# The first seven microseconds of a fused attention and mixer kernel: warm-up, tile 0 and the first weights rearranged

## The chip, the cores and the metric

The kernel runs on one core of a Trainium2 chip. A core has a matrix engine (TensorE; PE in the profile, with its weight loads as PEld), a vector engine (VectorE, DVE), a scalar engine (ScalarE, ACT), a general engine (GpSimd, POOL) and a sync engine (SyncE, SP), which here only issues DMAs. Each engine works through its own instructions in order and waits on semaphores for the others. Sixteen DMA engines move data. SBUF is the on-chip memory of 128 partitions, PSUM the accumulator memory of eight banks that TensorE writes. The metric is the time of one execution on the device in microseconds; lower is better.

## The reference

The input x has 2048 rows of 512 numbers in bf16. Each row is normalised (xn), and two branches work on xn; the output is x plus both.

```python
xn = layernorm(x)
# A: 32 heads of 16; each position attends to 8 positions, 2 apart, backwards
q, k, v = split(xn @ wqkv)
out_A = softmax(q . k[s - 2w] * 0.25 over w = 0..7) . v[s - 2w]  @ wo
# B: gated mixer with 688 + 688 channels
z = gelu(xn @ w_in);  z1 = z[:, :688];  z2 = layernorm(z[:, 688:])
g = w_sp @ z2 + b_sp[:, None]          # w_sp is 2048 x 2048
out_B = (z1 * g) @ w_out
return x + out_A + out_B
```

## The kernel before

The 2048 rows are 16 tiles of 128. The order of each engine's instructions is written out by hand, in five lists of short names (`pe`, `act`, `dve`, `pool`, `sp`) at the end of the kernel; `op_(name, after, f)` says what a name does and what it comes after, and the tile framework puts in the semaphore waits. No planner reorders anything.

**Front, per tile i.** SP loads x (`x0` to `x12`, line 163; tiles 0 to 5 one by one, then 2, 4 and 4 tiles). VectorE takes the statistics (`b`, line 170; `ag`, line 173), GpSimd turns the variance into a reciprocal root in two instructions (`gr`, lines 176 and 177), VectorE normalises (`n`, line 180; tile 0 in two halves of columns `n0a`, `n0`, line 184). For tiles 0 to 7 TensorE transposes xn in four 128x128 pieces into a bank of PSUM (`T`, line 213), ScalarE copies it to SBUF (`Tc`, line 216), and TensorE multiplies it by the 688 columns of the input weights that belong to z2 (`z`, line 231: 2 halves of 344 columns, 4 pieces of the contraction each, so eight matmuls). ScalarE applies gelu (`h`, line 249). Tiles 8 to 15 are transposed by DMA from SP's queue (`t`, line 196).

Tile 0 is cut finer: `T0a` and `T0` transpose two pieces each, into one bank; `Tc0a` and `Tc0` copy them; `z0a` and `z0A` do the first half of the columns (contraction pieces 0, 1 and 2, 3), `z0B` the second half.

**PSUM.** Three double banks `mm` and two single ones `aux` are handed out in turn; a user waits for the reader of the one before it. The transposes use `aux`, the products `mm`.

**What comes first.** VectorE clears a tile of zeros `warm` (line 129) and some small ones; nine matmuls of that tile with itself (`wu`, line 455) run on TensorE before tile 0 is there. ScalarE's queue issues the z2 weights in two DMAs `wz0` and `wz1` (line 239), one for each half of the columns, 688 bytes a piece. A clear of two numbers of that weight tile (line 142) makes `wz0` wait for VectorE; `wz1` stands behind it in the same queue. GpSimd issues the DMA of the bias (`b16`, line 245). Its transpose `B` (line 459) and copy `Bc` (line 461) turn it into a column of 16 numbers per partition; `B` stands between `T7` and `z6` in TensorE's list. The first block of the spatial weights (`W0`, line 451) reuses the memory of the zeros and so waits for `wu`.

**After the front** TensorE does the first z1 products `y`, the rest of z2, then q, k and v (line 324), the rest of z1, the spatial product (`M`, line 467), and the two output products (lines 511, 516 and 523), while VectorE works through the attention of the heads.

Of the kernel before, what the change touches and what calls it, by code (L numbers as in the profile page):

```python
# [7 lines left out]
BF16 = mybir.dt.bfloat16  # L8
# [5 lines left out]
P = 128  # L14
S = 2048
D = 512
NT = S // P
# [3 lines left out]
W = 8  # L21
# [5 lines left out]
FH = 688  # L27
F = 2 * FH
FHALF = FH // 2
# [13 lines left out]
def kernel(  # L43
# [12 lines left out]
    nc = tc.nc  # L56
    V = nc.vector
    A = nc.scalar
    G = nc.gpsimd
    PE = nc.tensor  # L60
# [9 lines left out]
    ident = sb.tile([P, P], BF16, name="ident")  # L70
# [12 lines left out]
    b16 = sb.tile([NT, P], BF16, name="b16")  # L83
    b_col = sb.tile([P, NT], F32, name="b_col")
# [7 lines left out]
    w_z = [wts[:, C * (3 * D + n * FH):C * (3 * D + (n + 1) * FH)].rearrange("p (k f) -> p k f", k=C) for n in (1, 0)]  # L92
# [13 lines left out]
    z2 = z2_r[:].rearrange("p (i f) -> p i f", i=NT)  # L106
# [9 lines left out]
    wsp_r = [wsp_all[:, n * NT * 2 * P:(n + 1) * NT * 2 * P] for n in range(3)]  # L116
# [4 lines left out]
    ph.append([wsp_r[2], z1_r[:, NT * D:NT * D + PU // 2]])  # L121
    ph.append([wsp_r[2], wts[:, 0:PU // 2]])
    BUF = dict(zip([(c, th) for c in range(NC) for th in range(2)], (0, 1, 2, 0, 1, 3, 0, 1)))
    warm = wsp_r[0][:, 0:D]

    mm = [ps.tile([P, 2, D], F32, name=f"mm{n}") for n in range(3)]
    aux = [ps.tile([P, D], F32, name=f"aux{n}") for n in range(2)]

    V.memset(warm, 0.0)  # L129
    V.memset(mhalf[:], -0.5)  # L130
    V.memset(eps_t[:], EPS)
    G.memset(ident[:], 0.0)
# [6 lines left out]
        V.memset(k_c[c][0:H, :, 0, 0:HALO], 0.0)  # L139
    V.memset(vp[0:H, :, 0, 0:HALO], 0.0)  # L140

    V.memset(w_z[1][0:1, 0, 0:2], 0.0)

    wq_d = A_wqkv.rearrange("(k p) f -> p k f", p=P)
    wi_d = B_w_in.rearrange("(k p) f -> p k f", p=P)
# [4 lines left out]
    def op_(name, after, f):  # L150
        assert name not in do, name
        do[name], needs[name] = f, list(after)

    def tok(i):
        return f"Tc{i}" if i < NPE else f"t{i}"
# [45 lines left out]
    def psum(kind, writer, reader, after, f):  # L201
        pool = mm if kind == "mm" else aux
        n = len(ring[kind])
        t = pool[n % len(pool)]
        old = [ring[kind][n - len(pool)]] if n >= len(pool) else []
        ring[kind].append(reader)
        op_(writer, list(after) + old, lambda: f(t))
        return t

    def turn(i, t, cs=range(C)):  # L210
        pt = t[:].bitcast(BF16)[:, 0:D]
        for c in cs:
            PE.transpose(pt[:, c * P:(c + 1) * P], xn[i % 8][:, c * P:(c + 1) * P], ident[:])  # L213

    def turned(i, t, c0=0, c1=C):
        A.copy(xnT[:, c0:c1, i * P:(i + 1) * P], t[:].bitcast(BF16)[:, c0 * P:c1 * P].rearrange("p (c t) -> p c t", c=c1 - c0))  # L216

    def make_T0():
        t = psum("aux", "T0a", "Tc0", ["n0a"], lambda t: turn(0, t, (0, 1)))
        op_("T0", ["T0a", "n0"], lambda: turn(0, t, (2, 3)))  # L220
        op_("Tc0a", ["T0a"], lambda: turned(0, t, 0, 2))
        op_("Tc0", ["T0"], lambda: turned(0, t, 2, 4))

    def make_T(i):
        t = psum("aux", f"T{i}", f"Tc{i}", [f"n{i}"], lambda t: turn(i, t))
# [3 lines left out]
    def z_half(t, i, part, hh, kcs=range(C)):  # L229
        for kc in kcs:  # L230
            PE.matmul(t[:, hh, 0:FHALF], xnT[:, kc, i * P:(i + 1) * P], w_z[part][:, kc, hh * FHALF:(hh + 1) * FHALF],  # L231
                      start=(kc == 0), stop=(kc == C - 1))

    def z_part(t, i, part):
        for hh in range(2):
            z_half(t, i, part, hh)

    for hh in range(2):
        op_(f"wz{hh}", [], lambda hh=hh: A.dma_start(  # L239
            w_z[1][:, :, hh * FHALF:(hh + 1) * FHALF], wi_d[:, :, FH + hh * FHALF:FH + (hh + 1) * FHALF]))  # L240
    op_("wk", [], lambda: SP.dma_start(w_k, wq_d[:, :, D:2 * D]))
    op_("wq", [], lambda: SP.dma_start(w_q, wq_d[:, :, 0:D]))
    op_("wv", [], lambda: SP.dma_start(w_v, wq_d[:, :, 2 * D:3 * D]))
# [3 lines left out]
    def z2_gelu(i, t):  # L247
        total = {"accum_out": zsum[:, i:i + 1]} if i in ZACT else {}
        A.activation(z2[:, i, :].rearrange("p (a b) -> p a b", a=2), t[:, :, 0:FHALF], ACT.Gelu_apprx_tanh, **total)  # L249
# [1 line left out]
    ZACT = range(8, NT)  # L251

    def make_z(i):
        t = psum("mm", f"z{i}", f"h{i}", [tok(i), "wz0", "wz1"], lambda t: z_part(t, i, 1))
        op_(f"h{i}", [f"z{i}"], lambda: z2_gelu(i, t))

    def make_z0():
        t0 = psum("mm", "z0a", "h0", ["Tc0a", "wz0"], lambda t: z_half(t, 0, 1, 0, (0, 1)))
        op_("z0A", ["z0a", tok(0)], lambda: z_half(t0, 0, 1, 0, (2, 3)))
        op_("z0B", ["z0A", "wz1"], lambda: z_half(t0, 0, 1, 1))  # L260
        op_("h0", ["z0B"], lambda: z2_gelu(0, t0))

    def z2_bn(i):
        for hh in range(2):
# [36 lines left out]
    for i in range(NT):  # L301
        g = i // 4 * 4
# [47 lines left out]
    last = {}  # L350
# [25 lines left out]
    for c, th in BUF:  # L376
        n = f"{c}{th}"
# [63 lines left out]
    USES = [f"y{i}" for i in range(NT)] + [f"{a}{p}" for a in "qkv" for p in range(8)]  # L441
# [8 lines left out]
    def load_wsp(n):  # L450
        SP.dma_start_transpose(wsp[n % 3], B_w_sp[n * 2 * P:(n + 1) * 2 * P, :])

    for n in range(8):
        op_(f"W{n}", [["wu"], [], ["HW"]][n] if n < 3 else [f"M{2 * n - 5}"], lambda n=n: load_wsp(n))
    op_("wu", [], lambda: [PE.matmul(aux[1][:], warm[:, 0:P], warm, start=True, stop=True) for _ in range(9)])

    def make_B():
        def turn_b(t):
            PE.transpose(t[:].bitcast(BF16)[:, 0:NT], b16[:], ident[0:NT, 0:NT])
        t = psum("aux", "B", "Bc", ["b16"], turn_b)  # L460
        op_("Bc", ["B"], lambda: A.copy(b_col[:], t[:].bitcast(BF16)[:, 0:NT]))

    def mix(t, j):
        w = wsp[(j // 2) % 3]
# [22 lines left out]
    def load_wo(g):  # L487
        SP.dma_start(wo_r[32 * g:32 * g + 32], A_wo.rearrange("(h d) n -> h d n", d=DH))
# [4 lines left out]
            SP.dma_start(wout[r:r + FREST, MF, :], B_w_out[MF * P:FH, :])  # L493

    for g in range(4):
        op_(f"LO{g}", [n for n in USES if n[0] != "y"] + [f"z{i}" for i in range(1, NT)] + ["z0B", last[3]], lambda g=g: load_wo(g))
    op_("LO4", USES, load_wout)
    LO = [f"LO{g}" for g in range(5)]
    for th in range(2):
# [59 lines left out]
    for n, c in enumerate(halves):  # L559
        i = groups[3][3]  # L560
# [1 line left out]
        op_(f"Sl{n}", [f"Fl{n}"], lambda n=n, c=c: (SP, A)[n].dma_start(out2[i * P:(i + 1) * P, c], o_of(i)[:, c]))  # L562


    pe = """wu T0a T0 z0a z0A T1 z0B T2 z1 T3 z2 T4 z3 T5 z4 T6 z5 T7 B z6 z7 y0 y1 z8 z9 z10 z11 z12 z13 z14
        k0 k1 q0 q1 z15 k2 k3 q2 q3 k4 k5 q4 q5 k6 k7 q6 q7
        v0 v1 v2 v3 v4 v5 v6 v7 y2 y3 y4 y5 y6 y7 y8 y9 y10 y11 y12 y13 y14 y15
        M0 M1 M2 M3 M4 M5 M6 M7 M8 M9 M10 M11 M12 M13 M14 M15
# [1 line left out]
    for n in pe:  # L570
        a, x = n[0], n[1:]
        if n in do:
            continue
        if n == "T0a":
            make_T0()
        elif a == "T":
            make_T(int(x))
        elif n == "z0a":
            make_z0()
        elif a == "z":  # L580
            make_z(int(x))
        elif a == "y":
            make_y(int(x))
        elif a in "qkv":
            make_heads(a, int(x))
        elif a == "M":
            make_M(int(x))
        elif a == "B":
            make_B()
    op_("GL", [], lambda: A.preload_act_table(ACT.Gelu_apprx_tanh))  # L590
    op_("EL", ["yg15"], lambda: A.preload_act_table_set("natural_log_exp_and_others"))

    act = """wz0 wz1 GL Tc0a Tc0 Tc1 Tc2 h0 Tc3 h1 Tc4 h2 Tc5 h3 Tc6 h4 Tc7 Bc h5 h6 h7 yg0 yg1 h8 h9 sq8 h10 h11 sq9 h12 h13 h14 sq10
        kc0 sq11 kc1 qc0 sq12 qc1 h15 kc2 sq13 kc3 sq14 qc2 sq15 qc3 kc4 kc5 qc4 qc5 kc6 kc7 qc6 qc7
        vc0 zn8 vc1 zn9 vc2 zn10 vc3 zn11 vc4 zn12 vc5 zn13 vc6 zn14 vc7 zn15
        yg2 yg3 yg4 yg5 yg6 yg7 yg8 yg9 yg10 yg11 yg12 yg13 yg14 yg15 EL
        G0 e0 G1 i0 e1 G2 i1 G3 G4 G5 G6 G7 G8 G9 G10 G11 G12 G13 G14 G15""".split()
    act += [f"E{i}" for n in (0, 1) for i in groups[n]]
    dve = """b0 ag0 b1 ag1 n0a n0 b2 ag2 n1 b3 ag3 n2 b4 ag4 n3 b5 ag5 n4 b6 ag6 b7 n5""".split()
    for i in range(6, NT):  # L600
        dve += [f"ag{i + 1}"] * (i + 1 < NT) + [f"b{i + 2}"] * (i + 2 < NT) + [f"n{i}"]
    dve += """zt0 zt1 zt2 zt3 zt4 zt5 zn0 zn1 zn2 zn3 zt6 zt7 zn4 zn5 zn6 zn7
# [62 lines left out]
```

## Time and profile before

| | us |
|---|---|
| median of three runs | 201.43 |
| lowest and highest of the three | 201.35, 202.9 |
| the profiled execution, whole | 201.17 |
| its span, first to last instruction | 199.4 |
| TensorE busy in the span | 194.3 |
| VectorE busy | 177.5 |
| ScalarE busy | 89.7 |
| GpSimd busy | 39.0 |

The span leaves out what comes before the first and after the last instruction, which is why it is shorter than the profiled execution. Times in the timeline count from the start of the span. In a row of the timeline the first number is the start, the second the length; what follows an arrow in square brackets is what ended the idle time before the instruction. A row with x4 stands for four instructions of one kind next to each other. Matmuls are pipelined, so a row's length includes the drain of its last one, and rows of TensorE overlap.

### The profile page before, as it was taken

To read this page: it belongs to the slowest core of one execution; us is meant where nothing else is said; L and a number is where in the kernel's file an instruction comes from. 1 tells how busy PE (TensorE), PEld (TensorE's weight loads), DVE (VectorE), ACT (ScalarE), POOL (GpSimd) and SP (SyncE) were. 2 spreads that over 40 slices of the span, in tenths; PEclk is the share of its full clock that TensorE was granted. 3 is DMA by queue.
4 is the path that set the end of the run, shared out by engine and by line. 5 is a ranking of instruction groups with operands and counts; after the bars stand their busy time and mean duration, and the time that the engine had idled before them with its cause. 6 is when DMAs were issued, how large, how long until landed. Compare 5 with 4: busy or idle time off the path is not lost.

```text
span 199.4 us, 4530 instructions
## 1 busy us (share of the span) xinstructions
PE 194.3 (97%) x1935; PEld 122.5 (61%) x1935; DVE 177.5 (89%) x204; ACT 89.7 (45%) x130; POOL 39.0 (20%) x67
## 2 busy tenths in 40 slices
PE   7899999999999999999999999999999999999993
PEld 2576666666777766666666666666666654443441
DVE  4999895899898999988999999999999999997234
ACT  2597797795559996672542311112221110043000
POOL 5677122002999330330000000000000000000000
PEclk9999999999999999999999999999999999999999
DMA  5999476840977999998099999999996679914233
GB/s 163 349 361 230 89 123 139 144 81 0 196 132 140 197 196 147 185 167 168 11 234 229 188 168 227 237 123 258 198 230 60 118 219 233 154 19 133 81 105 105
DMA packets 68964, 32.58 MB, mean 163 GB/s; under 512 B 56912, under 2 KB 67024, under 8 KB 68816
## 3 DMA queue, kind: packets, MB, share of 16 engines
q1 hardware_dynamic: 65568, 24.12, 59.5%
q0 software_dynamic: 2176, 7.40, 20.0%
q10 hardware_dynamic: 1200, 0.77, 1.4%
q8 instruction: 15, 0.25, 0.5%
q14 instruction: 5, 0.04, 0.1%
HBM read 10.03 MB, written 2.10 MB: 61 GB/s over the span
## 4 chain that ended last, share of the span: by engine, by line
PE 95%; DMA 3%; DVE 1%; ACTq 0%; DVEq 0%; issue 0%
PE mm L467 37%; PE mm L324 21%; PE mm L231 19%; PE mm L523 7%; PE mm L511 7%; DMA wts<-in_B_w_in_dram 3%; PE aux L511 2%; PE mm L516 1%; PE aux L213 1%; ACTq L239 0%; DVE z L561 0%; DVEq L660 0%; DVE wsp L129 0%; PE aux L523 0%; DVE qk L139 0%
## 5 line engine op out<-in xcount | busy, mean ns | idle before, releaser
L467 PE MATMUL mm<-z,wsp 128*128 128x344 bf16 x512 | 74.8, 309 | 0.0
L467 PEld LDWEIGHTS <-wsp 128*128 128x128 bf16 x512 | 50.1, 98 | 24.6
L324 PE MATMUL mm<-xnT,wts 128*32 128x512 bf16 x768 | 41.9, 380 | 0.0
L231 PE MATMUL mm<-wts,xnT 128*128 128x344 bf16 x256 | 39.0, 309 | 0.5 <-ACT xnT L216 0.5
L324 PEld LDWEIGHTS <-wts 128*32 128x32 bf16 x768 | 29.5, 140 | 12.0 <-issue 0.6
L425 DVE TENSOR_TENSOR prod<-vp,a_sb 128x4096 bf16<-128x4096 bf16 x16 | 36.1, 2285 | 0.0
L481 ACT ACTIVATE qk<-mm,b_col 128x688 bf16<-128x688 f32 x16 | 13.3, 830 | 45.3 <-PE mm L467 38.3
L231 PEld LDWEIGHTS <-xnT 128*128 128x128 bf16 x256 | 24.4, 98 | 13.0 <-issue 1.0
L358 DVE TENSOR_TENSOR prod<-qk 128x4096 bf16<-128x4096 bf16 x12 | 27.0, 2288 | 1.8 <-DMA qk<-qk 1.6
L429 DVE TENSOR_TENSOR prod<-prod,prod 128x8192 bf16<-128x8192 bf16 x6 | 26.5, 4420 | 0.0
L337 ACT CAST qk<-mm 128x1024 bf16<-128x1024 f32 x16 | 16.2, 1012 | 7.8 <-PE mm L324 7.8
L313 ACT ACTIVATE z<-mm 128x688 bf16<-128x688 f32 x16 | 11.8, 748 | 5.7 <-PE mm L231 5.3
L366 POOL DMA_DIRECT2D prod<-prod x10 | 8.7, 1022 | 28.3 <-DVE zvar L282 16.0
L523 PE MATMUL mm<-wts,xnT 32*128 32x512 bf16 x192 | 14.2, 374 | 0.0
L511 PEld LDWEIGHTS <-qk 128*128 128x128 bf16 x85 | 8.2, 98 | 9.4 <-issue 0.8
L511 PE MATMUL mm<-wts,qk 128*128 128x512 bf16 x60 | 13.6, 379 | 0.0
L249 ACT ACTIVATE z<-mm 128x688 bf16<-128x688 f32 x16 | 11.9, 745 | 1.9 <-PE mm L231 1.8
L170 DVE BATCH_NORM_STATS2 stats<-z 128x6 f32<-128x512 bf16 x16 | 10.8, 673 | 1.7 <-DMA z<-in_A_x_dram 1.7
L523 PEld LDWEIGHTS <-xnT 32*128 32x128 bf16 x256 | 6.3, 93 | 7.7 <-issue 0.8
L556 DVE TENSOR_TENSOR z<-mm,wsp 128x512 bf16<-128x512 f32 x6 | 3.8, 684 | 8.0 <-PE mm L523 4.8
L550 ACT CAST z<-mm 128x512 bf16<-128x512 f32 x6 | 3.2, 598 | 13.7 <-PE mm L523 12.3
L177 POOL TENSOR_TENSOR rstd<-rstd,mhalf 128x1 f32<-128x1 f32 x16 | 9.0, 561 | 1.3
(82 smaller groups left out, 169.6 us busy)
## 6 DMA issues: line engine op xcount, KB each, us to landing
prod<-prod POOLq DMA_DIRECT2D x10, 512.0 KB, 7.6
wts<-in_A_wo_dram SPq DMA_DIRECT2D x4, 512.0 KB, 6.3
wsp<-in_A_x_dram SPq DMA_DIRECT2D x2, 1024.0 KB, 6.5
out_dram<-z SPq DMA_DIRECT2D x15, 128.0 KB, 1.8
wts<-in_A_wqkv_dram SPq DMA_DIRECT2D x3, 512.0 KB, 8.6
z<-in_A_x_dram SPq DMA_DIRECT2D x2, 512.0 KB, 6.4
wsp<-z POOLq DMA_DIRECT2D x2, 512.0 KB, 6.5
wsp<-wts POOLq DMA_DIRECT2D x2, 512.0 KB, 8.9
```

What stands on the lines that cost most here:

```text
L231: PE.matmul(t[:, hh, 0:FHALF], xnT[:, kc, i * P:(i + 1) * P], w_z[part][:, kc, hh * FHALF:(hh + 1) * FHALF], start=(kc == 0), stop=(kc == ...
L249: A.activation(z2[:, i, :].rearrange("p (a b) -> p a b", a=2), t[:, :, 0:FHALF], ACT.Gelu_apprx_tanh, **total)
L313: op_(f"yg{i}", [f"y{i}"], lambda: A.activation(z1u[:, i, 0:FH].rearrange("p (a b) -> p a b", a=2), t[:, :, 0:FHALF], ACT.Gelu_apprx_tanh))
L324: PE.matmul(t[32 * g:32 * g + 32, dd, :], w, r, start=(kc == 0), stop=(kc == C - 1), tile_position=(0, 32 * g))
L337: op_(f"{a}c{p}", [f"{a}{p}"], lambda: A.copy(home(a, p), t[:].rearrange("p d (t s) -> p d t s", t=2)))
L358: V.tensor_tensor(pr, q, k, ALU.mult)
L425: return lambda: V.tensor_tensor(dst, vp[:, :, th, off:off + GS], a_sb[:, th, W - 1 - w].unsqueeze(1).broadcast_to([P, DH, GS]), ALU.mult)
L429: return lambda: V.tensor_tensor(dst, dst, x, ALU.add)
L467: PE.matmul(t[:, hh, 0:FHALF], w[:, k, (j % 2) * P:(j % 2 + 1) * P], z2[:, k, hh * FHALF:(hh + 1) * FHALF], start=(k == 0), stop=(k == NT ...
L481: lambda: A.activation(gs[j % 3].rearrange("p (a b) -> p a b", a=2), t[:, :, 0:FHALF], ACT.Identity, bias=b_col[:, j:j + 1]))
L511: PE.matmul(po[i][:, c], uT[th][:, m, t0:t0 + P], wout[:, m, c], start=(start and m == 0), stop=(stop and m == MF - 1))
L523: PE.matmul(po[groups[n][g]], op[32 * g:32 * g + 32, th, d, s * P:(s + 1) * P], wo_r[32 * g:32 * g + 32, d, :], start=(start and d == 0), ...
```

## The change

- **Warm-up.** The tile of zeros and its clear go. The warm-up multiplies a constant of ones that the framework holds, one number per partition read with stride zero, ten times instead of nine. Three more such products, of 128 columns (`wd`), come after tile 0's transposes. `W0` no longer comes after `wu`.
- **Tile 0 in two banks.** `T0a` and `T0` write one `aux` bank each, and `Tc0a` and `Tc0` read one each.
- **z2's weights by rows.** `wz0` brings contraction pieces 0 and 1 of all 688 columns, `wz1` pieces 2 and 3: pieces of 1376 bytes. `z0a` now does pieces 0 and 1 of both halves of columns, `z0b` pieces 2 and 3. The clear that holds the weights covers 128 partitions by 512 columns of the first piece.
- **Bias.** `B` stands right behind `T0`, ahead of `wd` and `z0a`, and uses a bank of `mm`; `Bc` stands behind `Tc0`. The products `z1` to `z15` come after `Bc`.
- **VectorE's list.** `b3 ag3 n2` becomes `b3 n2 ag3`.

```diff
-    warm = wsp_r[0][:, 0:D]
+    ones = nc.const_aps.tensor(1.0, [P, D], BF16)
...
-    V.memset(warm, 0.0)
...
-    V.memset(w_z[1][0:1, 0, 0:2], 0.0)
+    V.memset(w_z[1][:, 0, 0:D], 0.0)
...
-        t = psum("aux", "T0a", "Tc0", ["n0a"], lambda t: turn(0, t, (0, 1)))
-        op_("T0", ["T0a", "n0"], lambda: turn(0, t, (2, 3)))
-        op_("Tc0a", ["T0a"], lambda: turned(0, t, 0, 2))
-        op_("Tc0", ["T0"], lambda: turned(0, t, 2, 4))
+        t0 = psum("aux", "T0a", "Tc0a", ["n0a"], lambda t: turn(0, t, (0, 1)))
+        t1 = psum("aux", "T0", "Tc0", ["T0a", "n0"], lambda t: turn(0, t, (2, 3)))
+        op_("Tc0a", ["T0a"], lambda: turned(0, t0, 0, 2))
+        op_("Tc0", ["T0"], lambda: turned(0, t1, 2, 4))
...
-    for hh in range(2):
-        op_(f"wz{hh}", [], lambda hh=hh: A.dma_start(
-            w_z[1][:, :, hh * FHALF:(hh + 1) * FHALF], wi_d[:, :, FH + hh * FHALF:FH + (hh + 1) * FHALF]))
+    for n in range(2):
+        op_(f"wz{n}", [], lambda n=n: A.dma_start(w_z[1][:, 2 * n:2 * n + 2, :], wi_d[:, 2 * n:2 * n + 2, FH:F]))
...
-        t = psum("mm", f"z{i}", f"h{i}", [tok(i), "wz0", "wz1"], lambda t: z_part(t, i, 1))
+        t = psum("mm", f"z{i}", f"h{i}", [tok(i), "wz0", "wz1", "Bc"], lambda t: z_part(t, i, 1))
...
-        t0 = psum("mm", "z0a", "h0", ["Tc0a", "wz0"], lambda t: z_half(t, 0, 1, 0, (0, 1)))
-        op_("z0A", ["z0a", tok(0)], lambda: z_half(t0, 0, 1, 0, (2, 3)))
-        op_("z0B", ["z0A", "wz1"], lambda: z_half(t0, 0, 1, 1))
-        op_("h0", ["z0B"], lambda: z2_gelu(0, t0))
+        t0 = psum("mm", "z0a", "h0", ["Tc0a", "wz0"], lambda t: [z_half(t, 0, 1, hh, (0, 1)) for hh in range(2)])
+        op_("z0b", ["z0a", tok(0), "wz1"], lambda: [z_half(t0, 0, 1, hh, (2, 3)) for hh in range(2)])
+        op_("h0", ["z0b"], lambda: z2_gelu(0, t0))
...
-        op_(f"W{n}", [["wu"], [], ["HW"]][n] if n < 3 else [f"M{2 * n - 5}"], lambda n=n: load_wsp(n))
-    op_("wu", [], lambda: [PE.matmul(aux[1][:], warm[:, 0:P], warm, start=True, stop=True) for _ in range(9)])
+        op_(f"W{n}", [[], [], ["HW"]][n] if n < 3 else [f"M{2 * n - 5}"], lambda n=n: load_wsp(n))
+
+    def spin(t, cols, count):
+        for _ in range(count):
+            PE.matmul(t[:, 0:cols], ones[:, 0:P], ones[:, 0:cols], start=True, stop=True)
+
+    op_("wu", [], lambda: spin(aux[1], D, 10))
+    op_("wd", ["T0"], lambda: spin(mm[1][:, 0, :], P, 3))
...
-        t = psum("aux", "B", "Bc", ["b16"], turn_b)
-        op_("Bc", ["B"], lambda: A.copy(b_col[:], t[:].bitcast(BF16)[:, 0:NT]))
+        t = mm[2][:, 0, :]
+        op_("B", ["b16", "T0"], lambda: turn_b(t))
+        op_("Bc", ["B"], lambda: A.copy(b_col[:], t.bitcast(BF16)[:, 0:NT]))
...
-    pe = """wu T0a T0 z0a z0A T1 z0B T2 z1 T3 z2 T4 z3 T5 z4 T6 z5 T7 B z6 z7 y0 y1 z8 z9 z10 z11 z12 z13 z14
+    pe = """wu T0a T0 B wd z0a T1 z0b T2 z1 T3 z2 T4 z3 T5 z4 T6 z5 T7 z6 z7 y0 y1 z8 z9 z10 z11 z12 z13 z14
...
-    act = """wz0 wz1 GL Tc0a Tc0 Tc1 Tc2 h0 Tc3 h1 Tc4 h2 Tc5 h3 Tc6 h4 Tc7 Bc h5 h6 h7 yg0 yg1 h8 h9 sq8 h10 h11 sq9 h12 h13 h14 sq10
+    act = """wz0 wz1 GL Tc0a Tc0 Bc Tc1 Tc2 h0 Tc3 h1 Tc4 h2 Tc5 h3 Tc6 h4 Tc7 h5 h6 h7 yg0 yg1 h8 h9 sq8 h10 h11 sq9 h12 h13 h14 sq10
...
-    dve = """b0 ag0 b1 ag1 n0a n0 b2 ag2 n1 b3 ag3 n2 b4 ag4 n3 b5 ag5 n4 b6 ag6 b7 n5""".split()
+    dve = """b0 ag0 b1 ag1 n0a n0 b2 ag2 n1 b3 n2 ag3 b4 ag4 n3 b5 ag5 n4 b6 ag6 b7 n5""".split()
```

More of the change, by code (lines that the diff above doesn't have):

```diff
@@ L453 @@
     for n in range(8):
-        op_(f"W{n}", [["wu"], [], ["HW"]][n] if n < 3 else [f"M{2 * n - 5}"], lambda n=n: load_wsp(n))
-    op_("wu", [], lambda: [PE.matmul(aux[1][:], warm[:, 0:P], warm, start=True, stop=True) for _ in range(9)])
+        op_(f"W{n}", [[], [], ["HW"]][n] if n < 3 else [f"M{2 * n - 5}"], lambda n=n: load_wsp(n))
[4 more added lines that the diff above has]
+    op_("wd", ["T0"], lambda: spin(mm[1][:, 0, :], P, 3))
     def make_B():
         def turn_b(t):
-            PE.transpose(t[:].bitcast(BF16)[:, 0:NT], b16[:], ident[0:NT, 0:NT])
-        t = psum("aux", "B", "Bc", ["b16"], turn_b)
-        op_("Bc", ["B"], lambda: A.copy(b_col[:], t[:].bitcast(BF16)[:, 0:NT]))
+            PE.transpose(t.bitcast(BF16)[:, 0:NT], b16[:], ident[0:NT, 0:NT])
+        t = mm[2][:, 0, :]
+        op_("B", ["b16", "T0"], lambda: turn_b(t))
+        op_("Bc", ["B"], lambda: A.copy(b_col[:], t.bitcast(BF16)[:, 0:NT]))
     def mix(t, j):
@@ L495 @@
     for g in range(4):
-        op_(f"LO{g}", [n for n in USES if n[0] != "y"] + [f"z{i}" for i in range(1, NT)] + ["z0B", last[3]], lambda g=g: load_wo(g))
+        op_(f"LO{g}", [n for n in USES if n[0] != "y"] + [f"z{i}" for i in range(1, NT)] + ["z0b", last[3]], lambda g=g: load_wo(g))
     op_("LO4", USES, load_wout)
```

## The prediction

> **What bounds the kernel now.** I read the page first, then the chain of waits in order of time, then who made TensorE wait, and last the timeline of the first 13 us, where the change lies. The page:
>
> ```profile
> span 199.4 us, 4530 instructions
> PE 194.3 (97%) x1935; PEld 122.5 (61%) x1935; DVE 177.5 (89%) x204; ACT 89.7 (45%) x130; POOL 39.0 (20%) x67
> PE 95%; DMA 3%; DVE 1%; ACTq 0%; DVEq 0%; issue 0%
> ```
>
> TensorE is busy 194.3 of 199.4 us and 95% of the chain is its own work. A cut in the front is worth what it takes off the start of TensorE's unbroken work, no more. The chain (start, length, what) shows where that starts:
>
> ```profile
> 1.97 5.26 DMA wts<-in_B_w_in_dram
> 7.27 0.74 PE mm L231 x4
> 8.01 0.37 PE aux L213 x4
> ...
> 15.11 0.22 PE aux L213 x4
> ...
> 184.55 3.77 PE mm L523 x65
> ```
>
> ```profile
> 15.33 0.11 PE aux L459
> 15.45 5.65 PE mm L231 x38
> ```
>
> ```profile
> PE mm L231 <- ACT xnT L216: 0.5, 1, 0.5
> ```
>
> The second weight transfer lands at 7.23 and releases z0B at 7.27; from there the chain is TensorE alone. The wait of 0.5 is z0a's, for the copy of tile 0. The bias transpose (L459) is 0.11 us of the solid part. The chain makes the weights look like the limit. The timeline of the front corrects this (start, length, engine, line):
>
> ```profile
> 0.86 0.27 DVE L129 MEMSET wsp<- 128x256 uint32 x1 [0.86 <-PEq L649]
> ...
> 1.19 4.02 PE L455 MATMUL aux<-wsp 128*128 128x512 bf16 x9 [1.19 <-DVE wsp L129]
> ...
> 1.39 0.06 DVE L142 MEMSET wts<- 1x1 uint32 x1
> ...
> 1.67 0.68 POOL L245 DMA_DIRECT2D b<-in_B_b_sp_dram  x1
> ...
> 4.80 0.60 DVE L184 TENSOR_SCALAR z<-z,mv,rstd 128x256 bf16<-128x256 bf16 x2 [0.20 <-POOL rstd L177]
> ...
> 5.20 0.54 PE L213 MATMUL aux<-ident,z 128*128 128x128 bf16 x4
> ...
> 5.32 0.69 DVE L170 BATCH_NORM_STATS2 stats<-z 128x6 f32<-128x512 bf16 x1
> 5.78 0.65 ACT L216 COPY xnT<-aux 128x256 bf16<-128x256 bf16 x2 [1.97 <-PE aux L213]
> ...
> 6.14 0.38 DVE L180 TENSOR_SCALAR z<-z,mv,rstd 128x512 bf16<-128x512 bf16 x1
> ...
> 6.21 0.76 PE L231 MATMUL mm<-wts,xnT 128*128 128x344 bf16 x4 [0.46 <-ACT xnT L216]
> ...
> 6.65 0.55 POOL L177 TENSOR_TENSOR rstd<-rstd,mhalf 128x1 f32<-128x1 f32 x1
> ...
> 6.72 0.69 DVE L170 BATCH_NORM_STATS2 stats<-z 128x6 f32<-128x512 bf16 x1 [0.20 <-DMA z<-in_A_x_dram]
> ...
> 7.45 0.18 DVE L173 BATCH_NORM_AGGREGATE mv<-stats 128x2 f32<-128x6 f32 x1
> 7.55 0.38 DVE L180 TENSOR_SCALAR z<-z,mv,rstd 128x512 bf16<-128x512 bf16 x1
> ...
> 7.85 0.69 DVE L170 BATCH_NORM_STATS2 stats<-z 128x6 f32<-128x512 bf16 x1
> ...
> 7.99 0.40 PE L213 MATMUL aux<-ident,z 128*128 128x128 bf16 x4
> 8.06 0.55 POOL L177 TENSOR_TENSOR rstd<-rstd,mhalf 128x1 f32<-128x1 f32 x1
> ...
> 8.67 0.39 DVE L180 TENSOR_SCALAR z<-z,mv,rstd 128x512 bf16<-128x512 bf16 x1
> ...
> 9.39 0.39 PE L213 MATMUL aux<-ident,z 128*128 128x128 bf16 x4
> ...
> 9.79 0.39 DVE L180 TENSOR_SCALAR z<-z,mv,rstd 128x512 bf16<-128x512 bf16 x1
> ...
> 11.50 0.40 DVE L180 TENSOR_SCALAR z<-z,mv,rstd 128x512 bf16<-128x512 bf16 x1
> ...
> 12.17 0.39 PE L213 MATMUL aux<-ident,z 128*128 128x128 bf16 x4
> ...
> 14.87 11.09 SPq L196 DMA_TRANSPOSE xnT<-z  x8
> ```
>
> Tile 2's normalisation n2 (DVE, 7.55) ends at 7.93 and T2 starts at 7.99, 0.06 behind it. So T2 waits for VectorE: weights that land earlier only move the idle time from before z0B to before T2. VectorE in turn is held by x's third tile: b3 starts at 6.72 after waiting 0.20 for a DMA. The front has two chains that end together; the change shortens TensorE's, and touches VectorE's in two places.
>
> **The change part by part.**
>
> *Warm-up and clears.* The clear of the warm-up tile (0.27) goes; the clear that holds the weights grows from one word (0.06) to the same 128x256 words as the one that goes, so I price it at 0.27. The last clear ended at 1.45 and now ends at about 1.45 - 0.27 + 0.21 = 1.39: the weights' issue moves by less than 0.1, which I take as nothing. Ten spins cost 4.02 x 10/9 = 4.47 in place of 4.02, but need no clear: if TensorE starts when VectorE did, at 0.86, they end at 5.33, against T0a at 5.20. T0a may be 0.13 late, which the slack below takes up. No row has spins on a constant that is read with stride zero: bounds are nothing, and, were each to take twice as long, 4.5 us; I take nothing, as the row of 512 columns is nearest.
>
> *Two banks.* The copy of tile 0 starts at 5.78, after all four transposes (5.20 + 0.54). With a bank of its own the first half can follow the first pair, about 0.27 sooner, and z0a could start at 5.94 in place of 6.21. But B is now queued ahead of it on TensorE, and waits for the bias:
>
> ```profile
> b<-in_B_b_sp_dram POOLq DMA_DIRECT2D x1, 4.0 KB, 4.2
> ```
>
> It was issued at 1.67 and landed at about 5.87. Behind B in TensorE's queue stand the three short spins of wd (128 columns each, priced from four transposes in 0.22 of the chain: 0.17) and then z0a: 5.87 + 0.05 + 0.11 + 0.17 = 6.20. So the banks give nothing while the bias lands at 5.87; wd and the moved B cost nothing. Bounds: 0.27 gained if the bias came at 5.5, as much lost if it came at 6.1.
>
> *Weights by rows.* The queue tables of two stretches, 3.3 to 6.5 us (weights and x together) and 9.6 to 10.7 us (only packets of 1376 B), give packets, MB and share of 16 engines:
>
> ```profile
> q10 hardware_dynamic: 1007, 0.67, 69.9%
> q1 hardware_dynamic: 399, 0.37, 35.2%
> ```
>
> ```profile
> q1 hardware_dynamic: 315, 0.43, 106.3%
> ```
>
> The first pair adds up to over 100%: the engines are full. A 688 B packet takes 0.699 x 16 x 3.2 / 1007 = 35.5 ns, one of 1376 B 1.063 x 16 x 1.1 / 315 = 59.4 ns. 1024 of the former are now 512 of the latter: 36.4 - 30.4 = 6.0 us of engine time, 0.37 us over 16 engines. So what shares the engines with them, x2 and x3, and the weights, may land up to 0.37 sooner: wz1 at 6.86 to 7.23, x3 at 6.3 to 6.7. z0b starts at 6.20 + 0.59 (four of the eight matmuls of 1.17 us) + T1 0.22 = 7.01 or later and needs 0.59, so it ends about 7.6, ahead of T2.
>
> *VectorE's order b3 n2 ag3.* Let N be n2's start. With ag3 out of the way it follows b3 by 0.73 (6.72 to 7.45): 7.45 if x3 doesn't come sooner, against 7.55. Its other bound is GpSimd's root, done at 7.20, so 7.26. Hence N is 7.26 to 7.45. But ag3 now stands behind n2, 0.30 later (7.55 to 7.85), and n3 needs its result through GpSimd: ag3 at 7.45 to n3 at 8.67 is 1.22, of which GpSimd's root ends at 8.61. So n3 = N + 0.30 + 1.22 = N + 1.52, where it was n2 + 1.12: **VectorE now waits 0.30 for the root of tile 3.** Everything after it on VectorE is shifted: n4 = N + 2.64, n5 = N + 4.35 (9.79 to 11.50 is 1.71).
>
> TensorE: T2 = N + 0.44. T3 by its own work T2 + 1.40 = N + 1.84, by n3 N + 1.52 + 0.39 + 0.06 = N + 1.97, so it waits 0.13. T5 by work N + 1.97 + 2 x 1.39 = N + 4.75, by n5 N + 4.35 + 0.40 + 0.06 = N + 4.81. From there lookahead on VectorE covers it. T5 was at 12.17; it will be at 12.07 (N = 7.26) to 12.26 (N = 7.45): -0.10 to +0.09.
>
> *B out of the solid part.* -0.11 after T7, as nothing else waits there. The DMA transpose t8 leaves SP's queue behind n8, up to 0.3 later than 14.87; its landing in the worst of the eight:
>
> ```profile
> DMA to landing us min/median/max: 2.4/2.6/4.7
> ```
>
> 14.87 + 4.7 + 0.3 = 19.87, and z8 starts after 32 of the 38 matmuls, at 15.45 + 4.76 = 20.2. It holds by 0.2 to 0.3. The last work of VectorE that TensorE waits for has room too:
>
> ```profile
> 178.41 2.29 DVE L438 TENSOR_TENSOR xnT<-prod 128x4096 bf16<-128x4096 bf16 x1
> ```
>
> It ends at 180.70, ao2 starts at 184.55. W0's wait on the spins, which had long been over, is worth nothing.
>
> **Sum:** -0.10 to +0.09, less 0.11: -0.21 to -0.02. I take the middle, N = 7.36, since how the saved 0.37 is split between the weights and x isn't visible: **-0.12 us**. The profiled execution took 201.17 (span 199.4 and 1.8 around it), so 201.05; the median of the three runs is 201.43, 0.26 above it, so **201.3** for a median. Three runs spread by 1.55 us, so about 1% (2 us) is what a measurement can tell from no change, and this is far inside it.
>
> **The rivals.**
>
> *x pushed behind the weights (slower).* Place: b2 and b3. b2 starts at 5.32 with no room, and T1 to T5 hang on it. If the doubled packets win the engines, x2 comes after wz1. Worst case: wz1 lands at 7.23 - 0.37, less the 256 packets of x2 and x3 that went ahead (0.352 x 16 x 3.2 / 399 = 45 ns, 0.72 us in all), at 6.14; x2 0.36 after it, 6.50; b2 then at 6.53, 1.21 late, ag2 and N with it: N = 7.26 + 1.21 = 8.47, T5 at 13.28, sum +1.0. It decides from N above 7.47, that is from x3 0.02 later than now or x2 0.2 later. Against it: the total gets shorter and x2 stands first in its queue. I take +0.4: 201.8. [...]
>
> *The clock comes late (slower).* Nine spins of 512 columns took 0.45 each, while eight matmuls of 344 columns take 1.17, which is 0.22 for 512: the spins ran at about half rate, and z0a (four in 0.76, last drain included) at full rate. If another stretch as long as the warm-up (4.0 us) ran at half rate, it would cost at most 2.0, less the idle time in it: 1 to 2, I take 1.5, giving 202.8. The highest run of before, 202.9, would fit, without being shown to be this. For it: B waits for the bias, so TensorE still pauses between T0 and z0a. Against it: the spins start earlier and wd fills. [...]
>
> *TensorE's chain is what counts (faster).* If n3 doesn't wait, T3 follows T2 by 1.40: 7.70 against 7.99 gives -0.29 - 0.11 = -0.40: 201.0. Against it: n3's 1.22 behind ag3 is measured.
>
> **How the numbers follow.** Forecast 0.62, x behind the weights 0.17, late clock 0.11, TensorE's chain 0.10. The range takes in all but the late clock and the end of the x case, and the 0.26 between a profile and a median: 200.8 to 202.4. Slower by over 1% would need the clock case at its worst with x late too: 0.04. Faster by over 1% has no case: 0.01. Within 1%: 0.95.
>
> **What would show it.** n2 at 7.26 to 7.45, then VectorE idle about 0.3 before n3, released by GpSimd's root (L176 in the new file); TensorE waiting before T3; z0a at about 6.2 behind the bias; no bias transpose between T7 and z6; weights landing by 6.9; the whole below 201.4 by a tenth or two. It is wrong if spins with stride zero run slower than 0.45, if x2 lands after 5.5, or if z0a's rate is that of the spins.

## The result and the profile after

| | before | after |
|---|---|---|
| median of 22 runs each, us | 201.53 | 201.19 |
| lowest, highest, us | 201.24, 202.9 | 200.83, 202.12 |
| mean of the 22, us | 201.79 | 201.19 |
| profiled execution, us | 201.17 | 200.92 |
| its span, us | 199.4 | 199.1 |

The ratio is 0.9965, with a 95% interval of 0.9948 to 0.9982: the change is faster by 0.35%, 0.34 us in the median, inside the range of 200.8 to 202.4, and within 1% as forecast. The forecast gain was 0.12 us. The two profiles differ by about twice that, 0.25, the medians by 0.34, and the means by more still, 0.60. So there are two questions: where the 0.25 comes from, and why the mean gains more than the profile. (Counts of executions below leave out three of the kernel before that were disturbed, at 230 us and more.)

The page of the changed kernel, with the span and the busy times:

```profile
span 199.1 us, 4537 instructions
...
PE 194.8 (98%) x1939; PEld 122.7 (62%) x1939; DVE 177.7 (89%) x203; ACT 89.8 (45%) x130; POOL 38.8 (19%) x67
```

TensorE is busy 0.5 us longer (four more matmuls and an earlier start) in a span 0.3 shorter. The chain of waits of the changed kernel up to 28 us (start, length, what; line numbers are those of the changed file):

```profile
1.64 3.79 DMA z<-in_A_x_dram
5.46 0.71 DVE stats L169
...
6.80 0.56 POOL rstd L176
7.38 0.42 DVE z L179
7.85 0.40 PE aux L212 x4
...
15.09 0.22 PE aux L212 x4
15.31 12.83 PE mm L230 x88
28.14 7.07 PE mm L321 x128
```

The weights no longer stand in the chain. What ends last before T2 is x's tile 2, then its statistics, root and normalisation, and from 7.85 the chain is TensorE. z6 starts at 15.31 where it started at 15.45. The first of the products for q, k and v (line 321 here, 324 before) start at 28.14; the same two pieces of the kernel before are:

```profile
15.45 12.94 PE mm L231 x88
28.38 7.07 PE mm L324 x128
```

So 0.14 us are won at z6 and 0.24 at 28 us. The 88 matmuls between are the same, but their piece is 0.11 shorter. From there to the end of the span it is 171.0 us in both.

VectorE in the changed kernel, from the timeline (start, length, line):

```profile
6.71 0.69 DVE L169 BATCH_NORM_STATS2 stats<-z 128x6 f32<-128x512 bf16 x1
7.38 0.41 DVE L179 TENSOR_SCALAR z<-z,mv,rstd 128x512 bf16<-128x512 bf16 x1
7.71 0.18 DVE L172 BATCH_NORM_AGGREGATE mv<-stats 128x2 f32<-128x6 f32 x1
...
8.50 0.18 DVE L172 BATCH_NORM_AGGREGATE mv<-stats 128x2 f32<-128x6 f32 x1
8.83 0.41 DVE L179 TENSOR_SCALAR z<-z,mv,rstd 128x512 bf16<-128x512 bf16 x1
```

n2 is at 7.38, inside the forecast 7.26 to 7.45. ag3 stands behind it and n3 starts at 8.83, which is N + 1.45 (forecast N + 1.52). VectorE idles between ag4 and n3, for 0.15 us (forecast about 0.30). TensorE of the changed kernel:

```profile
0.77 4.27 PE L455 MATMUL aux<-const-bfloat16-1.0 128*128 128x512 bf16 x10 [0.77 <-PEq L653]
5.14 0.54 PE L212 MATMUL aux<-ident,z 128*128 128x128 bf16 x4
5.73 0.18 PE L462 MATMUL mm<-ident,b 16*128 16x16 bf16 x1
...
6.03 0.74 PE L230 MATMUL mm<-wts,xnT 128*128 128x344 bf16 x4
...
7.85 0.40 PE L212 MATMUL aux<-ident,z 128*128 128x128 bf16 x4
...
9.30 0.40 PE L212 MATMUL aux<-ident,z 128*128 128x128 bf16 x4
...
12.13 0.40 PE L212 MATMUL aux<-ident,z 128*128 128x128 bf16 x4
```

T2 came at 7.85 (7.99 before), T3 at 9.30 (9.39), T5 at 12.13 (12.17): the 0.14 us won at T2 has shrunk to 0.04 by T5, because n3 and n5 are later. The other 0.20 is at the bias. TensorE between T7 and z6, before and then after:

```profile
14.95 0.39 PE L213 MATMUL aux<-ident,z 128*128 128x128 bf16 x4
15.27 0.18 PE L459 MATMUL aux<-ident,b 16*128 16x16 bf16 x1
15.38 0.32 PE L231 MATMUL mm<-wts,xnT 128*128 128x344 bf16 x1
```

```profile
14.92 0.39 PE L212 MATMUL aux<-ident,z 128*128 128x128 bf16 x4
15.15 0.60 PE L230 MATMUL mm<-wts,xnT 128*128 128x344 bf16 x3
```

From T7 to z6 it was 0.43 us and is 0.23. So the profiles' difference is 0.03 before T7 and 0.20 for the bias transpose. The chain has the same 0.2 in two parts: 0.11 as the transpose's own piece (15.33, shown in the prediction) and 0.11 in the piece behind it, 12.94 against 12.83.

The queue of the weights and that of x in the changed kernel, 3.3 to 6.5 us:

```profile
q10 hardware_dynamic: 516, 0.67, 61.2%
q1 hardware_dynamic: 435, 0.40, 40.1%
```

A packet of the weights takes 0.612 x 16 x 3.2 / 516 = 60.7 ns (forecast 59.4); the weights' share fell from 69.9% to 61.2%. x moved more in the same time here (40.1% against 35.2%), but not in the profile with VectorE's order put back (35.0%, beside 61.6% for the weights), so a gain for x isn't shown.

### The profile page after: what moved, and what is told of

It is laid out like the page before. It is cut to its first block, busy times and chain, and to the rows that moved or that the text cites. A ratio compares the mean times of both kernels' runs of the same rounds, so it can differ in the third digit from the quotient of the medians.

```text
span 199.1 us, 4537 instructions
## 1 busy us (share of the span) xinstructions
PE 194.8 (98%) x1939; PEld 122.7 (62%) x1939; DVE 177.7 (89%) x203; ACT 89.8 (45%) x130; POOL 38.8 (19%) x67
## 4 chain that ended last, share of the span: by engine, by line
PE 94%; DMA 2%; DVE 1%; POOL 0%; SPq 0%; issue 0%; DVEq 0%
PE mm L471 37%; PE mm L321 21%; PE mm L230 18%; PE mm L527 7%; PE mm L515 7%; PE aux L515 2%; DMA z<-in_A_x_dram 2%; PE mm L520 1%; PE aux L212 1%; SPq L162 0%; DVE stats L169 0%; POOL rstd L176 0%; DVE z L565 0%; DVE z L179 0%; DVEq L664 0%
```

## The experiments

Twelve kernels ran, each twelve times (the last one six times), beside executions of the kernel before. Theory M says that the gain is the moved bias transpose; rival W that it is the warm-up, through executions in which TensorE's clock comes late. What W predicts is counted as executions over 202.2 us, a limit that was chosen after the first results: the kernel before has 23 of 118 in all, 21 of them between 202.6 and 203.0. Below, "typical" is the mean of the executions under that limit; for the kernel before it lies between 201.35 and 201.52 from one group of runs to the next, so each kernel is held against those that ran beside it.

### The changed kernel again

> The changed kernel once more, beside the three below. Theory M (the moved bias transpose): its profile stands 0.25 us below that of before, 0.20 of it from the gap between T7's last transpose and z6's first matmul, 0.03 from the front. Rival W (the warm-up): the median of several runs gains more than the profile does, 0.35 us or more, because single executions of the kernel before are long by up to 1.5 us and those of this one are not.

Measured: median 201.20, ratio 0.9964 (0.9943 to 0.9985); no execution over 202.2 (highest 201.56), while 7 of 35 of the kernel before were. The profiled execution took 200.85. The mean is 201.20, against 201.72 of the kernel before with its long executions and 201.45 without. The result repeats, and so does the gap between the two gains: W is alive.

### VectorE's order put back

```diff
-b3 n2 ag3 b4 ag4 n3
+b3 ag3 n2 b4 ag4 n3
```

> The changed kernel with VectorE's order b3 ag3 n2 put back. Theory M, with the prediction's arithmetic: n2 starts 0.1 later, T2 0.07 to 0.1 later, but n3 no longer waits for GpSimd and starts at about 8.6 in place of 8.83; T3 comes at about 9.32 (9.30 now), T5 at about 12.10 (12.13 now), so the whole differs from the changed kernel by less than 0.1 us. Rival: the 0.24 us for which VectorE waits before n3 is paid in full, so undoing it makes the whole 0.2 us faster than the changed kernel.

Measured: median 201.22, ratio 0.9964 (0.9943 to 0.9985), the same as the changed kernel. VectorE in its timeline:

```profile
7.02 0.69 DVE L169 BATCH_NORM_STATS2 stats<-z 128x6 f32<-128x512 bf16 x1 [0.23 <-DMA z<-in_A_x_dram]
...
7.84 0.38 DVE L179 TENSOR_SCALAR z<-z,mv,rstd 128x512 bf16<-128x512 bf16 x1
...
8.96 0.39 DVE L179 TENSOR_SCALAR z<-z,mv,rstd 128x512 bf16<-128x512 bf16 x1
```

n3 follows n2 by 1.12 again, without a wait (in the changed kernel VectorE waited 0.15 us there, not the 0.24 that the expectation names). Counted from b3, the swap brings n2 forward (0.67 in place of 0.82) and puts n3 back (2.12 in place of 1.94), so what it gains at n2 it loses at n3. x's tile 3 came at 7.0 here and at 6.7 in the changed kernel: this difference of 0.3 us between two profiles is more than any of the front's edits is worth.

### The old warm-up

```diff
-    ones = nc.const_aps.tensor(1.0, [P, D], BF16)
+    warm = wsp_r[0][:, 0:D]
...
+    V.memset(warm, 0.0)
...
-    op_("wu", [], lambda: spin(aux[1], D, 10))
-    op_("wd", ["T0"], lambda: spin(mm[1][:, 0, :], P, 3))
+    op_("wu", [], lambda: spin(aux[1], D, 9))
```

> The changed kernel with the old warm-up: nine matmuls of zeros behind the clear, no short ones behind tile 0. Theory M: nothing is lost, 0.2 to 0.3 us faster than before, as with the changed kernel. Rival W: the profile may be the same, but single executions are again long by 1 us and more, and the median gains 0.15 us less than that of the changed kernel.

Measured: median 201.86, ratio 1.001 (0.998 to 1.004), 4 of 12 over 202.2, highest 203.55. The whole gain is gone, although bias, banks, weights and order are the changed ones. But this edit did more than change the warm-up, and so it can't decide between M and W. Its chain and TensorE's wait:

```profile
2.88 4.79 DMA wts<-in_B_w_in_dram
```

```profile
7.71 0.74 PE L231 MATMUL mm<-wts,xnT 128*128 128x344 bf16 x4 [0.76 <-DMA wts<-in_B_w_in_dram]
```

The second half of the weights was issued at 2.88 us, in the changed kernel at 2.00: by the trace's record its issue now waits on the semaphore of x0, which landed at 2.86. It came at 7.67 (6.99 in the changed kernel), and T2 started at 8.29 in place of 7.85. That is about the 0.4 us by which even the eight executions under 202.2 are longer than the changed kernel's (201.58 against 201.20). How the loss divides between the weights and the warm-up isn't shown here.

### The bias alone

```diff
-        t = psum("aux", "B", "Bc", ["b16"], turn_b)
+        t = mm[2][:, 0, :]
+        op_("B", ["b16", "T0"], lambda: turn_b(t))
...
-    wu T0a T0 z0a z0A T1 ... z5 T7 B z6
+    wu T0a T0 B z0a z0A T1 ... z5 T7 z6
```

> The kernel before with the bias transpose and its copy alone moved (behind tile 0, own bank). Theory M: z6 follows T7 without a gap, 0.20 us earlier, and the whole gains 0.20 us; the prediction's price for this was 0.11. z0a is held by the bias by less than 0.1 us, which the wait for the weights takes up. Rival W: no more than 0.1 us.

Measured: median 201.51, ratio 0.9996 (0.997 to 1.0023); 4 of 12 over 202.2. The other eight have a mean of 201.37, against 201.45 of the 28 of the kernel before below 202.2 that ran beside them: 0.08 us, which this number of runs doesn't tell from 0.2 or from 0. The profile happened to be of one of the long executions (202.86) and shows what makes one long. TensorE in its timeline:

```profile
1.19 4.02 PE L455 MATMUL aux<-wsp 128*128 128x512 bf16 x9 [1.19 <-DVE wsp L129]
...
6.80 1.31 PE L231 MATMUL mm<-wts,xnT 128*128 128x344 bf16 x4 [0.75 <-DMA wts<-in_B_w_in_dram]
...
9.90 1.58 PE L231 MATMUL mm<-wts,xnT 128*128 128x344 bf16 x8
...
11.53 1.33 PE L231 MATMUL mm<-wts,xnT 128*128 128x344 bf16 x8
```

Four matmuls of 344 columns take 1.31 in place of 0.76, and only at 11.53 do eight take the 1.33 of a full clock. The warm-up was the usual nine, and the trace's record has the full clock from 10.39 us on, where the kernel before has it from 5.18. In the eleven profiles of executions under 202.2 us these four matmuls take 0.74 to 0.76; in the two with a late clock, this one and the one without a warm-up below, 1.31 and 1.33. The span is 201.1 us, 1.7 longer than that of the kernel before. Not all of it is the clock: the first weights came late too, and TensorE waited for them until 6.80 (6.21 before). Where T7 meets z6 the gap is gone here too (16.87 to 17.09), and the chain shows what that is worth:

```profile
16.87 0.39 PE L213 MATMUL aux<-ident,z 128*128 128x128 bf16 x4
17.09 0.75 PE L231 MATMUL mm<-wts,xnT 128*128 128x344 bf16 x4
```

```profile
17.03 0.22 PE aux L213 x4
17.26 12.83 PE mm L231 x88
30.09 7.07 PE mm L324 x128
```

From T7's piece to the products for q, k and v it is 13.06 us here and 13.27 in the kernel before (15.11 to 28.38). The other profiles agree: 13.27 in the one other kernel with the bias transpose between T7 and z6 (the warm-up alone), 13.05 or 13.06 in ten others, all with the transpose moved. From those products to the end of the span it is 171.0 us in every profile. So the move is worth 0.21 us, and all of it reaches the end; whatever else differs between these profiles arises before T7.

### The warm-up alone

```diff
-    V.memset(warm, 0.0)
...
+    op_("wu", [], lambda: spin(aux[1], D, 10))
+    op_("wd", ["T0"], lambda: spin(mm[1][:, 0, :], P, 3))
...
-    wu T0a T0 z0a
+    wu T0a T0 wd z0a
```

> The kernel before with the new warm-up alone (ten matmuls of ones without a clear, three short ones behind tile 0, the first load of spatial weights no longer behind them). Theory W (a longer and earlier warm-up makes a late clock rare): no execution over 202.2 us, where 7 of 35 of the kernel before are, so the mean gains 0.3 us or more; the typical execution is unchanged (201.2 to 201.4). Theory M (the bias alone): as before, long executions included.

Measured: median 201.35, none of 12 over 202.2 (highest 201.79), where 8 of 33 of the kernel before were; mean 201.42 against 201.72. The typical execution is as before: 201.39 is the mean of the 25 others of the kernel before. W holds: the long executions are gone, and nothing else is gained. Twelve executions alone would be few for that; the 94 of all kernels with ten matmuls, counted below, make it firm. (One thing moved with the edit: without the clear the weights are issued at 1.24 us in place of 1.48. In this profile x's tile 3 came late, and T2 only at 8.59.) From here to the changed kernel, 201.20, it is another 0.2 us.

### Without the short matmuls behind tile 0

```diff
-    op_("wd", ["T0"], lambda: spin(mm[1][:, 0, :], P, 3))
```

> The changed kernel without the three short warm-up matmuls behind tile 0. Theory W1 (ten matmuls from 0.77 us on are enough): as the changed kernel, median 201.2 us and none over 202.2. [...]

Measured: median 201.12, ratio 0.9968 (0.9946 to 0.999), none of 12 over 202.2. The three short matmuls do nothing that twelve executions show. In this profile the bias and x's tile 3 landed late: TensorE waited 0.40 us for the one, VectorE 0.43 for the other, and T2 came at 8.34.

### Ones in the old warm-up

```diff
-    V.memset(warm, 0.0)
+    V.memset(warm, 1.0)
```

(on the kernel with the old warm-up, nine matmuls)

> The changed kernel with the old warm-up (nine matmuls behind a clear, none behind tile 0), but the clear writes ones in place of zeros. If what is multiplied matters: as the changed kernel, median 201.2 us. If only the length and the start matter: as with zeros, median 201.7 to 202 us and a third of the executions over 202.2.

Measured: median 201.55, ratio 1.0006 (0.9975 to 1.0036), 3 of 12 over 202.2, all above 203. So ones behave as zeros did (4 of 12). As in the old warm-up with zeros, the second half of the weights is issued at 2.89, behind x0, and the clear of ones takes 0.48 us in place of 0.27; these two kernels can be held against each other, but not against the changed one.

### No warm-up

```diff
-    op_("wu", [], lambda: spin(aux[1], D, 10))
-    op_("wd", ["T0"], lambda: spin(mm[1][:, 0, :], P, 3))
+    op_("wu", [], lambda: spin(aux[1], P, 1))
```

> The changed kernel with a single matmul of 128 columns as warm-up and none behind tile 0. [...] If the warm-up were of no use: 201.2 us.

Measured: median 202.45, ratio 1.0027 (1.0001 to 1.0053), 8 of 12 over 202.2. So the warm-up is of use, as W has it: without it the median is 1.0 us above that of the kernel before (201.47) and 1.25 above that of the changed kernel. TensorE in its timeline:

```profile
5.24 0.65 PE L212 MATMUL aux<-ident,z 128*128 128x128 bf16 x4 [4.20 <-DVE z L183]
...
9.22 1.95 PE L230 MATMUL mm<-wts,xnT 128*128 128x344 bf16 x8
...
11.23 1.33 PE L230 MATMUL mm<-wts,xnT 128*128 128x344 bf16 x8
```

Before these, four such matmuls took 1.33 (from 6.09) and 1.35 us (from 7.64), where the changed kernel has 0.74. TensorE was busy 1.57 of 1.70 us from 5.20 and 3.30 of 3.30 from 7.00, and the full clock came within the eight matmuls from 9.22 (1.95 us in place of 1.33; at 10.47 by the trace's record). The profiled long execution of the bias alone, with nine matmuls and the full clock from 10.39, took 202.86 us, the profiled one here 202.56: there a warm-up after which the clock came late cost as much as none at all does here.

### Nine matmuls of ones

```diff
-    op_("wu", [], lambda: spin(aux[1], D, 10))
-    op_("wd", ["T0"], lambda: spin(mm[1][:, 0, :], P, 3))
+    op_("wu", [], lambda: spin(aux[1], D, 9))
```

> The changed kernel with nine long warm-up matmuls of ones in place of ten, and no short ones: they start at 0.77 us as in the changed kernel and are 3.8 us long as in the kernel before. If the length of unbroken work decides when the clock comes: executions over 202.2 us come back in about a quarter, as in the kernel before. If the early start decides: none, median 201.1 to 201.3 us, as with ten.

Measured: median 200.95, ratio 0.9987 (0.9961 to 1.0013), 2 of 12 over 202.2 (202.41 and 202.76). The six kernels with ten, the changed one twice, have none of 94; left out is the last one below, where the weights came late. The weights are issued as in the changed kernel (1.51 and 1.97). So the early start alone isn't enough; the tenth matmul counts, as far as two long executions can show it. 2 of 12 against 23 of 118 doesn't say whether the early start helps at all. Its other ten executions have the lowest mean of all kernels (200.98).

### The weights by columns

```diff
-        op_(f"wz{n}", [], lambda n=n: A.dma_start(w_z[1][:, 2 * n:2 * n + 2, :], wi_d[:, 2 * n:2 * n + 2, FH:F]))
+        op_(f"wz{hh}", [], lambda hh=hh: A.dma_start(
+            w_z[1][:, :, hh * FHALF:(hh + 1) * FHALF], wi_d[:, :, FH + hh * FHALF:FH + (hh + 1) * FHALF]))
```

> The changed kernel with the weights in two halves of columns again (688 B pieces), and z0 cut accordingly. The prediction's arithmetic: 0.37 us more of the DMA engines' time, so x3, the weights and n2 land up to 0.2 later: 0 to 0.2 us slower than the changed kernel, median 201.2 to 201.4. Rival (VectorE hides it): the same as the changed kernel.

Measured: median 201.33, mean 201.27 (the changed kernel's again 201.20), ratio 0.9989 (0.9969 to 1.001), none over 202.2. Against the typical execution of the kernel before beside it (201.35) its mean is 0.08 lower, that of the changed kernel 0.25 lower (201.45). Inconclusive: 0.07 to 0.17 us lies inside the scatter of twelve runs, and both expectations fit.

### Tile 0 in one bank

```diff
-        t0 = psum("aux", "T0a", "Tc0a", ["n0a"], lambda t: turn(0, t, (0, 1)))
-        t1 = psum("aux", "T0", "Tc0", ["T0a", "n0"], lambda t: turn(0, t, (2, 3)))
+        t = psum("aux", "T0a", "Tc0", ["n0a"], lambda t: turn(0, t, (0, 1)))
+        op_("T0", ["T0a", "n0"], lambda: turn(0, t, (2, 3)))
```

> The changed kernel with both halves of tile 0 in one bank. The prediction: the banks give nothing, since the bias holds z0a until about 6.0 and T2 waits for VectorE behind it: the same as the changed kernel within 0.1 us, median 201.1 to 201.3. Rival: z0a 0.25 later moves T1, z0b and T2 with it, 0.2 us slower.

Measured: median 201.02, ratio 0.9969 (0.9945 to 0.9993), none over 202.2: not slower than the changed kernel, as predicted. The copy of tile 0 starts later, and T2 still waits for VectorE. ScalarE's row and TensorE's:

```profile
5.80 0.65 ACT L215 COPY xnT<-aux 128x256 bf16<-128x256 bf16 x2 [2.02 <-PE aux L212]
```

```profile
5.99 0.18 PE L462 MATMUL mm<-ident,b 16*128 16x16 bf16 x1 [0.22 <-DMA b<-in_B_b_sp_dram]
```

The copy is 5.80 here and 5.46 with two banks, and B's wait for the bias covers the difference. (T2 came at 8.05, because x's tile 2 landed late: b2 at 5.66.)

### x's tile 2 through ScalarE's queue

```diff
+    V.memset(xs[0:1, 2, 0:2], 0.0)
...
-    act = """wz0 wz1 GL
+    act = """x2 wz0 wz1 GL
...
-b3 n2 ag3 b4
+b3 ag3 n2 b4
```

> The changed kernel with x's third tile issued from ScalarE's queue ahead of the weights (behind a clear of one word), and VectorE's order b3 ag3 n2. If x's landing is what bounds the front: b2 starts right behind n0 at 5.3, b3 at 6.4, n2 at 7.25 to 7.3, T2 at 7.7 and T3 at 9.1, 0.2 us before those of the changed kernel, median 201.0. If the weights, now issued 0.45 later, take over: the second half lands at 7.4, T2 comes at 8.05 and the whole is 0.1 to 0.2 us slower than the changed kernel.

Measured: 202.74 to 205.93 in six executions, median 203.95, ratio 1.01 (1.0054 to 1.0147). A failure, and not for the reason expected. Moving x2 changed which semaphore each DMA uses; the second weight DMA got the one of x0 and was issued only at 3.32 us, right behind x0's landing at 3.30, and came at 9.57. It is the accident of the old warm-up again. The profile is of the longest execution. Its chain of waits has both:

```profile
0.73 2.57 DMA z<-in_A_x_dram
...
3.32 6.25 DMA wts<-in_B_w_in_dram
```

TensorE, with the wait that this made:

```profile
9.62 1.30 PE L231 MATMUL mm<-wts,xnT 128*128 128x344 bf16 x4 [1.68 <-DMA wts<-in_B_w_in_dram]
...
11.14 2.50 PE L231 MATMUL mm<-wts,xnT 128*128 128x344 bf16 x8
```

and its stretches (from:to, length, PE busy, granted clock, DMA share, GB/s):

```profile
5.20:8.50 3.30, 1.87 (x16) 1.00 0.97 330
8.60:15.30 6.70, 5.68 (x26) 0.50 1.08 360
15.40:20.00 4.60, 4.60 (x41) 1.00 1.08 210
```

The clock had come and was full from 5.20 to 8.50 us (four matmuls in 0.74 from 6.97), while TensorE was busy 1.87 of 3.30 us; from 8.60 to 15.30 it was at half (0.50), and from 15.40 on full again. The trace's record has the changes at 8.55 and 15.38 us. Three of the other five executions have a mean granted clock of 0.992, two of 1.00, so in most of them, but not in all, the clock was below full for a part of the span. Whether an earlier x2 would have helped stays untested.

## Why the prediction was right, and where it was wrong

**Right.** The range also holds the median of the kernel before (201.53), so that the time lies in it says little; the forecast gain was 0.12 and the measured one 0.34. What was right is the account of the front. The reading that VectorE and x, not the weights, set T2: T2, T3 and T5 came within 0.06 us of the arithmetic with N = 7.38 (7.82, 9.35, 12.19 forecast; 7.85, 9.30, 12.13 measured). n3's wait for GpSimd appeared, and putting the order back changed nothing, as N + 0.44 against N + 1.97 says. Two banks gave nothing while the bias holds z0a. Packets of 1376 B took 60.7 ns. The weights landed by about 7.0; x did not gain from the saved 0.37 in this profile (b3, which works on what the prediction calls x's third tile, at 6.71 against 6.72), so the earlier N goes with the order. That N fell into its range of 7.26 to 7.45 is partly luck: in other profiles with ten matmuls and the same issue of x and the weights T2 came between 7.81 and 8.34, because x's tiles 2 and 3 landed at other times. Whether the rearranged front, the bias apart, gains anything is not shown.

**Wrong in size: "B out of the solid part, -0.11".** I took the chain's piece of 0.11 for the whole price. The starts of T7's and z6's matmuls show 0.20: B started 0.32 behind T7 and z6 0.11 behind B, where z6 alone now starts 0.23 behind T7. In the chain the other half stands in the piece behind it. With -0.21 in place of -0.11 the sum for N = 7.38 is -0.19, against 0.25 in the profiles. That the whole 0.21 reaches the end is shown by the profiles (13.27 against 13.05 or 13.06 us from T7 on, then 171.0 in all); the executions of the bias alone are too few for it (0.08, with scatter as large). The means point the same way. Against the typical execution of the kernel before beside them the warm-up alone is 0.03 longer; the changed kernel is 0.25 shorter, the order put back 0.22, no short matmuls 0.23, one bank 0.27 and the columns 0.08.

**Wrong in kind: "Warm-up and clears" prices the spins, and the sum has no term for what they are for.** The cost of ten spins was right: they took 4.27 and ended before T0a; that the weights' issue hardly moves was right too (1.48 to 1.51). The late clock stood among the rivals, as something that the change might meet (0.11, slower by 1.5). The one profiled long execution of a kernel with nine matmuls, that of the bias alone, shows it: half rate until 10.39 us. Executions as long as that were about one in five of the kernel before (23 of 118 over 202.2), 1 to 1.5 us each, and the changed kernel had none; that these too had a late clock is my inference. In the first 22 executions of each the long ones are 0.27 of the 0.60 us by which the mean fell (201.79 against 201.52 without the five long ones); the other 0.33 is the typical execution, 0.21 of it the bias transpose. Three runs of before with 202.9 among them were the hint, and I had noted it as one that "would fit" without drawing the conclusion.

Of the two other rivals, "TensorE's chain is what counts" didn't occur: n3 did wait. "x pushed behind the weights" didn't decide in the profile of the changed kernel, where x2 landed 0.14 later (b2 at 5.46 against 5.32), short of the 0.2 from which it does. In profiles with the same issue of x and the weights it did: b2 came at 5.63 without the short matmuls and at 5.66 with one bank. But it also came at 5.67 with the old 688-byte pieces (the bias alone), so that the bigger pieces are the cause isn't shown.

No version clearly beat the changed kernel: without the three short matmuls (201.12) and with one bank (201.02) it is as fast within the scatter, and both are simpler.

## What to carry to other kernels

Put a price on a warm-up by how many of many executions are long, and not by a profile of one; here nine matmuls in place of ten cost nothing in ten executions and 1.4 and 1.8 us in two (202.41 and 202.76, beside a mean of 200.98). Where two chains end together, work out what the later engine waits for after each edit: a result that is moved one place back in a queue (ag3) can be needed by the next tile through another engine. Read the price of an instruction in a solid stretch from the starts of its neighbours, not from its piece in the chain. And before an experiment's time is read, compare when its transfers were issued with the kernel that it is meant to differ from in one thing: the old warm-up also put off half of the weights by 0.9 us.

## What the runs showed of the hardware

- With ten matmuls of 512 columns from 0.77 us on (4.27 to 4.43 us), no execution of 94 (six kernels) was over 202.2 us. With nine (3.5 to 4.0 us) it was 2 of 12 with an early start and 27 of 130 behind a clear (the kernel before and the bias alone; 7 of 24 more in the two kernels with late weights). Zeros or ones made no difference (4 and 3 of 12). Between the kernel with nine from 0.77 us on (2 of 12) and the one without the short matmuls (none of 12) the difference is the tenth matmul, 0.43 us, as far as two long executions show it.
- In the profile of the kernel with x's tile 2 moved the clock, once granted, was taken back: it was full from 5.20 to 8.50 us, in which TensorE was busy 1.87 of 3.30 us and so not idle throughout, and 0.50 from 8.60 to 15.30. Four other long executions (203.56 of the kernel before, 203.36 and 203.55 with the old warm-up, 202.76 with nine matmuls of ones) have a mean granted clock of 0.992: 0.8% of 202 us is 1.6, which at a clock of 0.50 is 3.2 us of the span (an estimate). Other long executions have a mean of 1.00, the profiled one of the bias alone among them (202.86), although its first four products took 1.31 us in place of 0.76; so the mean doesn't show a late first grant, and long executions come in two kinds. None of the 94 is below 0.997.
- A constant read with stride zero runs as a warm-up at the same 0.43 us per 512 columns as the zeros of the kernel before: in both profiles the matmuls start 0.43 us apart.
- The landing of x's tiles varied from profile to profile of nearly the same front: b3 started at 6.58 with nine matmuls of ones and at 7.27, behind a wait for its tile, without the short matmuls, 0.7 us apart.
